# Head pairs, 128-key chunks and a hand-written issue order in a soft-cap attention followed by gated attention experts

## The chip, the cores and the metric

The kernel runs on one core of a Trainium2 chip, in one launch. The metric is the device time of an execution in microseconds (us). Most executions of a kernel agree within 0.3%. TensorE matmuls are called PE, its weight loads PEld, VectorE DVE, ScalarE ACT, GpSimd POOL and SyncE SP.

## The reference

q, k and v are (8, 12, 448, 64), batch, head, position, feature; the output is (8, 448, 768).

```
scores = (q @ k.T) / 8                       # per batch and head
scores = 30 * tanh(scores / 30)
x      = softmax(scores) @ v                 # heads side by side: (8, 448, 768)

logits = x @ w_gate                          # 4 experts, the best 2 of each token
w      = softmax over the two chosen logits
for e in range(4):
    qe, ke, ve = x @ wq[e], x @ wk[e], x @ wv[e]        # 64 wide
    a   = softmax(causal(qe @ ke.T / 8))
    out += (w of e, 0 where not chosen) * (a @ ve @ wo[e])
```

The first part is called stage A, the second stage B. All four experts are computed for all tokens; the weight of an expert that was not chosen is 0.

## The kernel before, in words

Positions go in four chunks of 112. Stage A has 96 iterations, one for a head (batch b, head h, t = 12 b + h). `a_prep` transposes q and k, padded from 64 to 96 features, in eight PE transposes into one PSUM tile, and DVE copies them out. `a_qkt` makes the scores with keys on the partitions: four matmuls of 448 query columns into a score tile of four PSUM banks, of which there is one. `a_tanh` and `a_exp` are one ACT activation each over 112 partitions x 1792 columns. `a_pv` runs 16 matmuls with 112x112 weights (the probabilities) and 65 moving columns (v and a column of ones, which gives the row sum), and DVE normalises.

Stage B of a batch is 18 closures in the list `bq`: x transposed and the gate (`b_xt_gate`), V of all experts (`b_vproj`), then per expert the projection (`b_proj`: Q and K side by side in 128 weight columns), the scores, the causal mask added by a second matmul, one exp over all 448 x 448 (`b_attn`, in the same score tile as stage A), and PV, normalising and the transpose of the result (`b_pv_o`), then four output blocks (`b_out`). They come into the list when the batch is done in stage A, and `pump_bq` takes one out in each iteration, two in every third:

```
        pump_bq(None, 2 if h % 3 == 1 else 1)
        a_qkt(t + 1)
        if t < NH:
            a_exp(t)
    while bq:
        pump_bq(None, 1)
```

PSUM has eight banks: four for the score tile, and four buffers of one bank each (`ps_aux`) which everything else shares. q, k and v of a batch are loaded by three DMAs from the GpSimd queue that convert f32 to f16 on the way (`load_batch`); the weights by 17 such DMAs ahead of them. Each engine takes its instructions in the order in which its queue has them. The functions stand here with the line numbers of the profile.

## Time and profile before

| | |
|---|---|
| median of three runs | 691.7 us (687.6 to 695.7) |
| span of the profiled execution | 686.8 us |
| PE / PEld / DVE / ACT / POOL busy | 538.4 / 408.7 / 261.1 / 372.9 / 124.1 us |
| mean granted TensorE clock | 0.767 |

The profiled execution's time is known by its span, from the first instruction to the last; the runs are timed from outside. PE's busy time is modelled, matmuls overlap in it, so spacings of starts are the safer reading. The granted clock is a share of 2.4 GHz; it takes two levels, 0.5 (1.2 GHz) and 1.0, and before the first recorded change the column shows 1.00 whatever the level.

### The profile page before, as it was taken

How to read it: one execution, taken by the hardware profiler on the slowest of the kernel's cores; microseconds unless marked ns; L12 is line 12 of the kernel's file. 1: busy time of each engine (PE TensorE's matmuls, PEld its weight loads, DVE VectorE, ACT ScalarE, POOL GpSimd, SP SyncE). 2: the span in 40 equal slices, each digit the busy share in tenths (PEclk: the TensorE clock that was granted, in tenths of full speed). 3: DMA queues.
4: the chain of work that ended last, by engine and by line, in shares of the span. 5: the costliest groups of instructions: out<-in, count | busy, mean ns of one | idle time of the engine just before them, and what ended most of it. 6: DMA issues, size and time to landing. Idle time of an engine off the chain costs nothing.

```text
span 686.8 us, 10320 instructions
## 1 busy us (share of the span) xinstructions
PE 538.4 (78%) x4416; PEld 408.7 (60%) x4416; DVE 261.1 (38%) x696; ACT 372.9 (54%) x233; POOL 124.1 (18%) x181
## 2 busy tenths in 40 slices
...
GB/s 80 105 128 22 59 64 1 1 73 112 18 1 52 59 93 1 0 91 72 42 2 81 40 82 1 82 41 21 62 1 1 0 21 62 0 0 81 1 0 81
DMA packets 144062, 29.76 MB, mean 43 GB/s; under 512 B 140177, under 2 KB 140433, under 8 KB 144017
## 3 DMA queue, kind: packets, MB, share of 16 engines
...
## 4 chain that ended last, share of the span: by engine, by line
PE 65%; ACT 17%; DVE 5%; POOL 4%; DMA 4%; issue 4%; DVEq 0%; POOLq 0%; ACTq 0%
PE score L143 13%; PE pv L176 13%; PE qkp L272 8%; ACT pTB L303 8%; PE wops L353 7%; ACT y L155 5%; PE scoreB L288 5%; ACT pT L163 5%; PE pvB L318 4%; PE tps L123 3%; PE tps L128 3%; PE vps L255 3%; PE otp L340 2%; DMA out_dram<-osb 2%; DMA k<-in_k_dram 2%
## 5 line engine op out<-in xcount | busy, mean ns | idle before, releaser
L155 ACT ACTIVATE y<-score 112x1792 f16<-112x1792 f32 x96 | 159.4, 1661 | 154.9 <-PE score L143 154.7
L163 ACT ACTIVATE pT<-y 112x1792 f16<-112x1792 f16 x96 | 162.6, 1694 | 2.0
L143 PE MATMUL score<-qkT 96*112 96x448 f16 x384 | 130.4, 473 | 32.7 <-ACT pTB L303 31.5
L176 PEld LDWEIGHTS <-pT 112*112 112x112 f16 x1536 | 125.2, 174 | 37.5 <-ACT pT L163 30.4
L176 PE MATMUL pv<-v,pT 112*112 112x65 f16 x1536 | 129.6, 251 | 12.0 <-ACT pT L163 11.9
L303 ACT ACTIVATE pTB<-scoreB 112x1792 f16<-112x1792 f32 x32 | 53.2, 1663 | 123.8 <-PE scoreB L295 123.8
L143 PEld LDWEIGHTS <-qkT 96*112 96x112 f16 x384 | 62.4, 175 | 62.7 <-issue 53.8
L187 DVE RECIPROCAL rcp<-pv 112x4 f32<-112x4 f32 x96 | 17.5, 183 | 202.7 <-PE pv L176 202.6
L123 PE MATMUL tps<-ident,q 112*96 112x112 f16 x384 | 69.7, 267 | 29.5 <-POOL v L103 29.5
L134 DVE COPY qkT<-tps 96x896 f16<-96x896 f16 x96 | 59.1, 616 | 48.4 <-PE tps L128 41.6
L123 PEld LDWEIGHTS <-q 112*96 112x96 f16 x384 | 58.2, 169 | 29.6 <-POOL v L103 29.5
L128 PE MATMUL tps<-ident,k 112*96 112x112 f16 x384 | 68.5, 264 | 4.5 <-DMA k<-in_k_dram 4.5
L278 POOL MEMSET qT<- 32x448 f16 x32 | 14.9, 464 | 294.8 <-PE scoreB L295 294.5
L272 PE MATMUL qkp<-xT,wqk 128*128 128x448 f16 x192 | 67.8, 516 | 0.0
L353 PE MATMUL wops<-wo,oT 96*112 96x384 f16 x256 | 64.3, 418 | 1.6 <-DVE osb L360 1.6
L128 PEld LDWEIGHTS <-k 112*96 112x96 f16 x384 | 58.8, 169 | 4.8 <-issue 4.8
L288 PE MATMUL scoreB<-qT,kT 96*112 96x448 f16 x128 | 39.3, 390 | 28.1 <-DVE kT L281 20.8
L318 PE MATMUL pvB<-vall,pTB 112*112 112x65 f16 x320 | 32.8, 268 | 23.1 <-ACT pTB L303 23.1
L353 PEld LDWEIGHTS <-oT 96*112 96x112 f16 x256 | 41.4, 171 | 15.2 <-issue 1.6
L318 PEld LDWEIGHTS <-pTB 112*112 112x112 f16 x320 | 30.3, 195 | 27.0 <-ACT pTB L303 27.0
L360 DVE COPY osb<-wops 112x384 f32<-112x384 f32 x64 | 35.0, 555 | 29.5 <-PE wops L353 21.5
L188 DVE TENSOR_TENSOR x<-pv,rcp 112x256 f16<-112x256 f32 x96 | 40.7, 424 | 3.2
...
## 6 DMA issues: line engine op xcount, KB each, us to landing
out_dram<-osb SPq DMA_DIRECT2D x32, 336.0 KB, 2.7
q<-in_q_dram POOLq DMA_DIRECT2D x8, 672.0 KB, 8.9
k<-in_k_dram POOLq DMA_DIRECT2D x8, 672.0 KB, 11.6
v<-in_v_dram POOLq DMA_DIRECT2D x8, 672.0 KB, 12.5
...
```

The lines of the kernel that those rows point to most:

```text
L123: nc.tensor.transpose(tps[0:KPAD, 0, c * CS : (c + 1) * CS], q16[:, h, c, 0:KPAD], ident[0:CS, 0:CS],)
L128: nc.tensor.transpose(tps[0:KPAD, 1, c * CS : (c + 1) * CS], k16[:, h, c, 0:KPAD], ident[0:CS, 0:CS],)
L134: nc.vector.tensor_copy(qkT[0:KPAD, :, :], tps[0:KPAD, :, :])
L143: nc.tensor.matmul(score[0:CS, kc, 0:S], qkT[0:KPAD, 1, kc * CS : (kc + 1) * CS], qkT[0:KPAD, 0, 0:S], start=True, stop=True,)
L155: nc.scalar.activation(yt[0:CS, :, :], score[0:CS, :, 0:S], AF.Tanh, scale=inv_scale_a / capf)
L163: nc.scalar.activation(pT[0:CS, :, :], yt[0:CS, :, :], AF.Exp, scale=capf)
L176: nc.tensor.matmul(pv[:, qc, 0 : Dh + 1], pT[0:CS, kc, qc * CS : (qc + 1) * CS], v16[:, h, kc, 0 : Dh + 1], start=(kc == 0), stop=(kc == N ...
L272: nc.tensor.matmul(qkp[:, :], wqk16[e][:, j, :], xT[:, j, :], start=(j == 0), stop=(j == NDC - 1),)
L288: nc.tensor.matmul(score[0:CS, kc, 0:S], st["kT"][0:KPAD, kc * CS : (kc + 1) * CS], st["qT"][0:KPAD, 0:S], start=True, stop=False,)
L303: nc.scalar.activation(pT[0:CS, :, :], score[0:CS, :, 0:S], AF.Exp, scale=inv_scale_a)
L318: nc.tensor.matmul(pv[:, qc, 0 : Dh + 1], pT[0:CS, kc, qc * CS : (qc + 1) * CS], vall[:, kc, e, 0 : Dh + 1], start=(kc == 0), stop=(kc == qc),
L353: nc.tensor.matmul(wops[:, :], otiles[(b, e)][0:KPAD, tcx * CS : (tcx + 1) * CS], wo16[e][0:KPAD, half * 384 : (half + 1) * 384], start=(e ...
```

## The change

Nearly the whole kernel is rewritten; what is computed stays. Stage A goes by pairs of heads (48 iterations): q and k of both heads lie side by side in 128 partitions, so eight transposes serve two heads. Keys go in three chunks of 128, and the last 64 keys of both heads share a fourth chunk, block-diagonal with zeros (`ktz`, `vtz`). The first group of a pair (`fill0`, `tanh(p, 0)`, `expo(p, 0)`) has four chunks, the second (`fill1`, ...) three. Query blocks are four windows of 128, the last of which overlaps the third by 64; all weights of PV are so 128 columns wide. x is transposed pair by pair in stage A (`a_xt`).

Stage B goes by two pairs of experts. Q, K and output weights are stacked 128 wide for a pair, V of all experts and the gate come in one product of 260 columns, and the scores are only computed and kept where a query can see a key: blocks of 448, 320 and 192 columns side by side, 1984 for a pair of experts, one exp over them. The steps of a batch stand in a table (`tab`) of eight iterations with two places in each: w1 ahead of the pair's second tanh, w2 at the iteration's end; steps 6 and 7 coincide with steps 0 and 1 of the next batch. The two iterations marked "S" put the packed scores and their exp between two halves of stage A's exp.

Loads become plain f32 DMAs from SP, one batch ahead, and GpSimd converts to f16 three pairs ahead (`a_cast`, seven copies a pair). The weights keep their converting DMAs, after the first casts. The scheduler is set to keep the written order (`manual_schedule`). PSUM: four banks of score, two for PV (`ps_pv`), and two buffers of one bank for all else (`ps_aux`), in place of four.

Cut to its core (removed lines are those of the functions above):

```diff
+    HP = H // 2
+    NP = B * HP
...
+    isc = 1.0 / (Dh ** 0.5)
+    QC, QP = 4, 112
+    KC, KM = 3, 384
+    TL = S - KM
+    WIN = (0, 128, 256, S - 128)
...
+    ps_pv = ctx.enter_context(tc.tile_pool(name="ps_pv", bufs=1, space=bass.MemoryType.PSUM))
+    ps_aux = ctx.enter_context(tc.tile_pool(name="ps_aux", bufs=2, space=bass.MemoryType.PSUM))
+    ctx.enter_context(tc.manual_schedule())
...
+    def load(b, groups):
...
+        for g0, gn in groups:
+            h0, h1 = 2 * g0, 2 * (g0 + gn)
+            nc.sync.dma_start(
+                qf[:, h0:h1, :], q[b, h0:h1].rearrange("h (p c) d -> p h (c d)", c=QC)
+            )
+            nc.sync.dma_start(
+                kf[:, h0:h1, :],
+                k[b, h0:h1, 0:KM].rearrange("h (p c) d -> p h (c d)", c=KC),
+            )
+            kt = k[b, h0:h1, KM:S].rearrange("(j two) p d -> two p j d", two=2)
+            nc.sync.dma_start(ktf[0:64, g0 : g0 + gn, :], kt[0])
+            nc.sync.dma_start(ktf[64:128, g0 : g0 + gn, :], kt[1])
+            nc.sync.dma_start(
+                vf[:, h0:h1, :],
+                v[b, h0:h1, 0:KM].rearrange("h (p c) d -> p h (c d)", c=KC),
+            )
+            vt_ = v[b, h0:h1, KM:S].rearrange("(j two) p d -> two p j d", two=2)
+            nc.sync.dma_start(vtf[0:64, g0 : g0 + gn, :], vt_[0])
+            nc.sync.dma_start(vtf[64:128, g0 : g0 + gn, :], vt_[1])
+        staged[b] = (qf, kf, vf, ktf, vtf)
+    load(0, [(0, 1), (1, 1), (2, 2), (4, 2)])
...
+    def a_cast(p):
...
+        k16 = hd.tile([128, KC, 2, Dh], f16, name=f"k16_{p}", tag="k16")
+        nc.gpsimd.tensor_copy(
+            q16, qf[:, h0 : h0 + 2, :].rearrange("p h (c d) -> p c h d", c=QC)
+        )
+        nc.gpsimd.tensor_copy(
+            k16, kf[:, h0 : h0 + 2, :].rearrange("p h (c d) -> p c h d", c=KC)
+        )
+        kt = ktz[b % 2]
+        nc.gpsimd.tensor_copy(kt[0:64, j, 0:Dh], ktf[0:64, j, :])
+        nc.gpsimd.tensor_copy(kt[64:128, j, Dh:128], ktf[64:128, j, :])
+        vv = v16[b % 2]
+        nc.gpsimd.tensor_copy(
+            vv[:, h0 : h0 + 2, :, 0:Dh],
+            vf[:, h0 : h0 + 2, :].rearrange("p h (c d) -> p h c d", c=KC),
+        )
+        vt_ = vtz[b % 2]
+        nc.gpsimd.tensor_copy(vt_[0:64, j, 0, 0:Dh], vtf[0:64, j, :])
+        nc.gpsimd.tensor_copy(vt_[64:128, j, 1, 0:Dh], vtf[64:128, j, :])
+        cast[p] = (q16, k16)
...
+    def a_tr(p):
...
+        for c in range(QC):
             nc.tensor.transpose(
+                tps[:, c * QP : (c + 1) * QP],
+                q16[:, c, :, :].rearrange("p h d -> p (h d)"),
+                ident[0:QP, 0:QP],
+            )
+        nc.tensor.transpose(tps[:, S : S + 128], ktz[b % 2][:, j, :], ident)
+        for c in range(KC):
             nc.tensor.transpose(
+                tps[:, S + 128 * (c + 1) : S + 128 * (c + 2)],
+                k16[:, c, :, :].rearrange("p h d -> p (h d)"),
+                ident,
+            )
+        qt = hd.tile([128, S + 128], f16, name=f"qt_{p}", tag="qt")
+        nc.vector.tensor_copy(qt, tps[:, 0 : S + 128])
+        kk = kz[p % 3]
+        nc.vector.tensor_copy(kk[0:64, 0, :], tps[0:64, S + 128 : S + 512])
+        nc.vector.tensor_copy(kk[64:128, 1, :], tps[64:128, S + 128 : S + 512])
+        qkt[p] = (qt, kk)
...
+    def fill0(p):
...
+                sc[:, c, 0:S], kk[:, 0, 128 * c : 128 * (c + 1)], qt[:, 0:S],
+                start=True, stop=True,
+            )
+        nc.tensor.matmul(sc[:, 3, 0:S], qt[:, S : S + 128], qt[:, 0:S], start=True, stop=True)
+        score[(p, 0)] = sc
+    def fill1(p):
...
+        for c in range(KC):
+            nc.tensor.matmul(
+                sc[:, c, 0:S], kk[:, 1, 128 * c : 128 * (c + 1)], qt[:, 0:S],
+                start=True, stop=True,
+            )
+        score[(p, 1)] = sc
+    y = {}
+    pr = {}
...
+    def tanh(p, g):
...
+        yt = actp.tile([128, n, S], f16, name=f"y{g}_{p}", tag=f"y{g}")
+        nc.scalar.activation(yt, sc[:, 0:n, 0:S], AF.Tanh, scale=isc / capf)
+        y[(p, g)] = yt
+    def expo(p, g, c0=None, c1=None):
+        n = 4 - g
+        yt = y[(p, g)]
+        if (p, g) not in pr:
+            pr[(p, g)] = actp.tile([128, n, S], f16, name=f"p{g}_{p}", tag=f"p{g}")
+        pt = pr[(p, g)]
+        c0 = 0 if c0 is None else c0
...
+    pvs = {}
...
+    def a_pv(p, g):
...
+        for n in range(4):
+            w = WIN[n]
+            for c in range(KC + 1):
+                if c < KC:
+                    lhsT = pt[:, c, w : w + 128]
+                    rhs = v16[b % 2][:, 2 * j + g, c, :]
+                else:
+                    lhsT = p0[:, KC, w : w + 128]
+                    rhs = vtz[b % 2][:, j, g, :]
                 nc.tensor.matmul(
+                    pv[:, g, 65 * n : 65 * n + 65], lhsT, rhs,
+                    start=(c == 0), stop=(c == KC),
                 )
...
+    def a_norm(p):
...
+        nc.vector.reciprocal(rc, pv[:, :, :, 64:65])
+        xk = hd.tile([128, 4, 2, Dh], f16, name=f"xk_{p}", tag="xk")
         nc.vector.tensor_tensor(
+            xk.rearrange("p n g d -> p g n d"),
+            pv[:, :, :, 0:64],
+            rc.broadcast_to((128, 2, 4, Dh)),
             ALU.mult,
         )
...
+    def a_xt(p):
...
+        transpose4(ps, lambda n: xk[:, n, :, :].rearrange("p g d -> p (g d)"))
+        nc.vector.tensor_copy(
+            xT[b][:, j, :].rearrange("m (p c) -> m c p", c=QC),
+            ps[:, 0:S].rearrange("m (c p) -> m c p", c=QC),
+        )
+    st = {}
...
+    def b_v(b, n):
...
+        ps = ps_aux.tile([128, E * Dh + E], f32, name=f"vps_{b}_{n}", tag="aux")
         for j in range(NDC):
+            nc.tensor.matmul(
+                ps, xT[b][:, j, WIN[n] : WIN[n] + 128], wvg[:, j, :],
+                start=(j == 0), stop=(j == NDC - 1)
+            )
+        pse = ps[:, 0 : E * Dh].rearrange("p (e d) -> p e d", d=Dh)
+        if n < 3:
+            nc.vector.tensor_copy(s["vall"][:, n, :, 0:Dh], pse)
+        else:
+            vb = vtB[b % 2]
+            nc.vector.tensor_copy(vb[0:64, 0:E:2, 0:Dh], pse[64:128, 0:E:2, :])
...
+    def b_q(b, r):
...
+        for j in range(NDC):
+            nc.tensor.matmul(
+                ps, wq2[r][:, j, :], xT[b][:, j, :], start=(j == 0), stop=(j == NDC - 1)
+            )
+        qe = bp.tile([128, S], f16, name=f"qe_{b}_{r}", tag="qe")
+        nc.vector.tensor_copy(qe, ps)
+        s["qe", r] = qe
+    def b_k(b, r):
+        ps = ps_aux.tile([128, S], f32, name=f"kps_{b}_{r}", tag="aux")
+        for j in range(NDC):
+            nc.tensor.matmul(
+                ps, wk2[r][:, j, :], xT[b][:, j, :], start=(j == 0), stop=(j == NDC - 1)
+            )
+        kk = kzB[r]
+        nc.vector.tensor_copy(kk[0:64, 0:S], ps[0:64, :])
+        nc.vector.tensor_copy(kk[64:128, S : S + TL], ps[64:128, KM:S])
+        nc.vector.tensor_copy(kk[64:128, S + TL : 2 * S], ps[64:128, 0:KM])
...
+    COL = {(0, 0): 64, (0, 1): 512, (0, 2): 832, (1, 1): 1024, (1, 2): 1344, (1, 0): 1536}
+    def b_fill(b, r):
+        qe = st[b]["qe", r]
+        kk = kzB[r]
+        sc = ps_score.tile([128, 2048], f32, name=f"sB_{b}_{r}", tag="score")
+        nc.tensor.matmul(sc[:, 0:64], kk[:, KM : KM + 128], qe[:, KM:S], start=True, stop=False)
+        nc.tensor.matmul(
+            sc[:, 0:64], ltm2, ident[:, 0:64], start=False, stop=True,
+        )
+        for (e, c), o in COL.items():
+            n = S - 128 * c
+            nc.tensor.matmul(
+                sc[:, o : o + n], kk[:, e * (S + TL) + 128 * c : e * (S + TL) + 128 * (c + 1)],
+                qe[:, 128 * c : S],
+                start=True, stop=False,
+            )
+            nc.tensor.matmul(sc[:, o : o + 128], ltm, ident, start=False, stop=True)
+        st[b]["sc", r] = sc
+    def b_exp(b, r):
+        s = st[b]
+        pb = pB[r]
+        nc.scalar.activation(pb[:, 64:2048], s.pop(("sc", r))[:, 0:1984], AF.Exp, scale=isc)
...
+    def b_pv1(b, e):
...
+        for n in range(4):
+            w = WIN[n]
+            cs = [c for c in range(KC) if 128 * c <= w] if n < 3 else list(range(KC))
+            ops = []
+            for c in cs:
+                o = 64 + COL[(g, c)] + w - 128 * c
+                ops.append((o, s["vall"][:, c, e, :]))
+            if n == 3:
+                ops.append((0, vtB[b % 2][:, e, :]))
+            for i, (o, rhs) in enumerate(ops):
+                nc.tensor.matmul(
+                    pv[:, n, :], pb[:, o : o + 128], rhs,
+                    start=(i == 0), stop=(i == len(ops) - 1),
                 )
+        rc = bp.tile([128, 4, 1], f32, name=f"rcB_{b}_{e}", tag="rcB")
+        nc.vector.reciprocal(rc, pv[:, :, Dh : Dh + 1])
+        sl = bp.tile([128, 4, 1], f32, name=f"sl_{b}_{e}", tag="sl")
+        nc.vector.tensor_tensor(sl, rc, s["wtok"][:, :, e : e + 1], ALU.mult)
+        nc.vector.tensor_tensor(
+            s["osc", r][:, :, g, :], pv[:, :, 0:Dh], sl.broadcast_to((128, 4, Dh)), ALU.mult
...
+    def b_ot(b, r):
...
+        transpose4(ps, lambda n: osc[:, n, :, :].rearrange("p g d -> p (g d)"))
+        oT = bp.tile([128, S], f16, name=f"oT_{b}_{r}", tag="oT", bufs=4)
...
+    def b_wo(b, n):
+        s = st[b]
+        w = WIN[n]
+        lo = 64 if n == 3 else 0
+        ob = outp.tile([128, D], f32, name=f"ob_{b}_{n}", tag="ob")
+        for f in range(2):
+            ps = ps_aux.tile([128, D // 2], f32, name=f"wops_{b}_{n}_{f}", tag="aux")
+            for r in range(2):
                 nc.tensor.matmul(
...
+                ob[lo:128, f * (D // 2) : (f + 1) * (D // 2)], ps[lo:128, :]
+            )
...
+        nc.sync.dma_start(out[b, w + lo : w + 128, :], ob[lo:128, :])
+    a_cast(0)
+    a_cast(1)
...
+    def weights(e):
...
+        nc.gpsimd.dma_start(
+            wk2[r][:, :, g * Dh : (g + 1) * Dh],
+            moe_wk[e].rearrange("(c p) m -> p c m", p=128),
+        )
+        nc.gpsimd.dma_start(wo2[r][g * Dh : (g + 1) * Dh, :], moe_wo[e])
+        if e == 0:
+            nc.gpsimd.dma_start(
+                wvg[:, :, E * Dh : E * Dh + E], moe_w_gate.rearrange("(c p) e -> p c e", p=128)
...
+    def batch_b(b):
...
+        tab = {
+            0: ([f(b_v, b, 0)], [f(b_v, b, 1), f(b_v, b, 2)]),
+            1: ([f(b_v, b, 3)], [f(b_gate, b), f(b_q, b, 0)]),
+            2: ([f(b_k, b, 0)], [("S", b, 0)]),
+            3: ([f(b_q, b, 1)], [f(b_k, b, 1)]),
+            4: ([f(b_pv1, b, 0), f(b_pv1, b, 1)], [("S", b, 1)]),
+            5: (
+                [f(b_pv1, b, 2), f(b_pv1, b, 3)],
+                [f(b_ot, b, 0), f(b_ot, b, 1), f(b_wo, b, 0)],
+            ),
+            6: ([f(b_wo, b, 1)], []),
+            7: ([f(b_wo, b, 2)], [f(b_wo, b, 3)]),
+        }
+        return tab
+    sched = {}
...
+        for s_, (w1, w2) in batch_b(b).items():
+            e_ = sched.setdefault(HP * (b + 1) + 1 + s_, ([], []))
+            e_[0].extend(w1)
+            e_[1].extend(w2)
+    def run(units):
+        for u in units:
+            u()
+    a_tr(0)
+    a_cast(2)
+    weights(0)
+    a_tr(1)
+    fill0(0)
+    last = max(sched)
+    for p in range(last + 1):
+        w1, w2 = sched.get(p, ([], []))
+        sB = [u for u in w2 if isinstance(u, tuple)]
+        w2 = [u for u in w2 if not isinstance(u, tuple)]
+        b, j = divmod(p, HP)
+        if j == 0 and b + 1 < B:
+            load(b + 1, [(0, HP)])
+        if p < NP:
+            tanh(p, 0)
+            fill1(p)
+        if 1 <= p <= NP:
+            expo(p - 1, 1)
+            a_pv(p - 1, 0)
+        a_tr(p + 2)
+        a_cast(p + 3)
+        if 1 <= p < 4:
+            weights(p)
+        run(w1)
+        if p < NP:
+            tanh(p, 1)
+        if not sB:
+            fill0(p + 1)
+            if p < NP:
+                expo(p, 0)
+        else:
+            for _, bb, r in sB:
+                b_fill(bb, r)
+            if p < NP:
+                expo(p, 0, 0, 2)
+            for _, bb, r in sB:
+                b_exp(bb, r)
+            fill0(p + 1)
+            if p < NP:
+                expo(p, 0, 2, 4)
+        if 1 <= p <= NP:
+            a_pv(p - 1, 1)
+            a_norm(p - 1)
+        run(w2)
+        if 1 <= p <= NP:
+            a_xt(p - 1)
```

## Rows read from the trace of the kernel before

**Rows 1.** The page: busy time of each engine; the chain that ended last.

```profile
PE 538.4 (78%) x4416; PEld 408.7 (60%) x4416; DVE 261.1 (38%) x696; ACT 372.9 (54%) x233; POOL 124.1 (18%) x181
...
PE 65%; ACT 17%; DVE 5%; POOL 4%; DMA 4%; issue 4%; DVEq 0%; POOLq 0%; ACTq 0%
```

**Rows 2.** Windows: stretch, length, busy us per engine (instructions), granted clock, DMA share, GB/s.

```profile
40.00:84.00 44.00, 43.92 (x331) 34.34 (x330) 13.53 (x34) 39.67 (x24) 11.06 (x14) 1.00 1.79 61
...
160.00:240.00 80.00, 68.08 (x594) 52.00 (x593) 34.06 (x93) 51.50 (x33) 15.73 (x21) 0.74 0.79 44
268.00:290.00 22.00, 18.72 (x121) 13.23 (x120) 6.48 (x16) 11.63 (x7) 3.50 (x6) 0.50 0.00 1
...
590.00:687.00 97.00, 58.19 (x355) 37.93 (x354) 31.80 (x83) 11.82 (x8) 5.64 (x16) 0.69 0.09 29
```

**Rows 3.** Timeline of PE, 56 to 66 us: start, us, instructions, count.

```profile
56.20 1.66 PE L176 MATMUL pv<-v,pT 112*112 112x65 f16 x16
57.68 0.31 PE L123 MATMUL tps<-ident,q 112*96 112x112 f16 x1
...
59.92 1.67 PE L176 MATMUL pv<-v,pT 112*112 112x65 f16 x16
```

**Rows 4.** Timelines of PE, 83.5 to 90 and 90 to 96 us.

```profile
84.50 1.33 PE L201 MATMUL xtp<-ident,x 112*128 112x112 f16 x12
...
92.77 1.30 PE L272 MATMUL qkp<-xT,wqk 128*128 128x448 f16 x6
93.91 0.92 PE L143 MATMUL score<-qkT 96*112 96x448 f16 x4
94.67 0.97 PE L176 MATMUL pv<-v,pT 112*112 112x65 f16 x16
95.48 0.23 PE L123 MATMUL tps<-ident,q 112*96 112x112 f16 x1
```

**Rows 5.** Groups of weight loads: shapes, count | busy, mean ns | idle before.

```profile
L201 PEld LDWEIGHTS <-x 112*128 112x128 f16 x192 | 12.8, 103 | 3.8 <-issue 1.5
L211 PEld LDWEIGHTS <-xT 128*112 128x112 f16 x192 | 12.7, 132 | 0.6
```

**Rows 6.** Groups of ACT, with what ended the idle time before.

```profile
L163 ACT ACTIVATE pT<-y 112x1792 f16<-112x1792 f16 x96 | 162.6, 1694 | 2.0
L155 ACT ACTIVATE y<-score 112x1792 f16<-112x1792 f32 x96 | 159.4, 1661 | 154.9 <-PE score L143 154.7
...
L219 ACT ACTIVATE eexp<-lg 112x16 f32<-112x16 f32 x8 | 1.5, 183 | 17.1 <-PE lg L211 17.1
```

**Rows 7.** Groups of DVE: three copies out of PSUM.

```profile
L134 DVE COPY qkT<-tps 96x896 f16<-96x896 f16 x96 | 59.1, 616 | 48.4 <-PE tps L128 41.6
...
L360 DVE COPY osb<-wops 112x384 f32<-112x384 f32 x64 | 35.0, 555 | 29.5 <-PE wops L353 21.5 <-DMA out_dram<-osb 6.9
...
L206 DVE COPY xT<-xtp 128x448 f16<-128x448 f16 x48 | 15.2, 379 | 0.8 <-PE xtp L201 0.7
```

**Rows 8.** Groups of POOL.

```profile
L101 POOL MEMSET q<- 112x1536 f16 x8 | 11.1, 1386 | 51.5 <-PE tps L123 29.5 <-PE tps L128 12.5 <-issue 9.4
...
L103 POOL MEMSET v<- 112x48 f16 x8 | 2.5, 318 | 28.3 <-PE pv L176 24.7 <-issue 3.5
...
masks.py:199 POOL TENSOR_SCALAR_AFFINE_SELECT ident<-ident 128x128 f16<-128x128 f16 x1 | 0.3, 287 | 0.1
...
L415 POOL MEMSET const-uint8-127<- 128x1 uint8 x1 | 0.1, 103 | 0.0
```

**Rows 9.** Timeline of ACT, from 560 us on.

```profile
587.35 1.69 ACT L163 ACTIVATE pT<-y 112x1792 f16<-112x1792 f16 x1
```

**Rows 10.** Timeline of ACT, first 40 us; the page: DMA issues.

```profile
37.83 1.66 ACT L155 ACTIVATE y<-score 112x1792 f16<-112x1792 f32 x1 [35.81 <-PE score L143]
...
out_dram<-osb SPq DMA_DIRECT2D x32, 336.0 KB, 2.7
...
v<-in_v_dram POOLq DMA_DIRECT2D x8, 672.0 KB, 12.5
```

More of the change, by code (lines that the diff above doesn't have):

```diff
@@ new lines @@
+    vtB = [const.tile([128, E, Dh + 1], f16, name=f"vtB{i}") for i in range(2)]
+    pB = [const.tile([128, 64 + 1984], f16, name=f"pB{i}") for i in range(2)]
+    for i in range(2):
+        nc.gpsimd.memset(ktz[i], 0.0)
+    for i in range(3):
+        nc.vector.memset(kz[i], 0.0)
+    for i in range(2):
+        nc.vector.memset(v16[i][:, :, :, Dh : Dh + 1], 1.0)
+        nc.vector.memset(vtz[i], 0.0)
+        nc.vector.memset(vtz[i][0:64, :, 0, Dh : Dh + 1], 1.0)
+        nc.vector.memset(vtz[i][64:128, :, 1, Dh : Dh + 1], 1.0)
```

482 lines of the change are left out of this document (152 added, 330 removed).

## The prediction, made before the changed kernel ran

> **What bounds the kernel now.** I read the chain first, then the stretches. The chain is 65% PE and 17% ACT, while PE is busy 538 of 687 us and ACT 373 [rows 1]: no engine is full over the whole span, so the stages must be looked at apart. From 40 to 84 us only stage A runs, and PE is busy 43.9 of 44 us, ACT 39.7 [rows 2]. A head takes 3.72 us from one PV to the next, and the 16 PV matmuls 1.48 us, 92 ns each [rows 3]; later the same 16 take 0.81 us, 51 ns each [rows 4]. So TensorE ran at the lower of its two levels (1.2 GHz) before and at the upper (2.4 GHz) after. The clock column of the first stretch says 1.00, but the spacing decides. From 160 to 240 us PE has 68 of 80 us, ACT 51.5, clock 0.74; at 268 to 290 us it is 0.50 with PE busy 18.7 of 22 [rows 2]. ACT's tanh waits 154.7 us for PE's scores [rows 6]. Two ends lie outside this: ACT's first tanh begins at 37.8 us [rows 10], and its last stage-A exp ends at 589.0 [rows 9], 97.8 us before the end; in 590 to 687 us ACT is busy 11.8 and PE 58.2 [rows 2]. That tail is the queue's backlog: 18 closures come in per batch, 16 are pulled.
>
> **ACT per pair.** Both activations cover 1792 columns. From 16 columns in 183 ns to 1792 in 1661 [rows 6] one column costs 0.832 ns and the rest 170 ns. A pair now has tanh over 1792 (1.66) and 1344 columns (170 + 1344 x 0.832 = 1.29), exp over 1792 (1.69) and 1344 (1.32): 5.96 us, where two heads took 6.71. 48 pairs: 286 us. Stage B's exp covers 1984 columns for two experts (1.82 us) in place of two of 1792 columns; the split exp beside it adds 0.17. Fourteen of the sixteen, and seven gate exps of 0.18, stand between stage-A work: 14 x 1.99 + 1.3 = 29 us.
>
> **PE.** Columns that stream, per pair: transposes 960, scores 7 x 448, PV 32 x 65, x transposes 512: 6,688. Per batch stage B adds 24 x 260 (V and gate), 2 x 5,376 (Q, K), 2 x 2,816 (packed scores and masks), 40 x 65, 1,024 and 16 x 384: 32,392. Six matmuls of 448 columns start 1.14 us before what follows, 190 ns each [rows 4], so the upper level is 2.36 columns per ns; the lower is half of it, 1.2. A pair costs 2.8 or 5.6 us, a batch with its stage B (72,520 columns) 30.7 or 60.4; ACT needs 6 x 5.96 + 2 x 1.99 + 0.18 = 39.9. PV goes by its weight loads: 112 columns in 92 ns is 1.2 per ns [rows 3]. But weights of 128 columns load in 103 ns where 112 take 132 [rows 5]. So I price the 128-wide PV by its 65 columns, 28 ns; the bound above is 53 ns (128 columns at 2.4 GHz), which adds 32 x 25 ns = 0.8 us a pair of PE time that ACT covers.
>
> The level decides. In rows it stayed low through 44 us of full PE on 96- and 112-wide tiles, and was up by 94.67 us, after the stretch with the 128-wide x transposes from 84.5 us [rows 2, 4]. Every tile of the new kernel is 112 or 128 rows by 128 columns, and stage A alone brings 6,688 columns in 5.96 us, 1,120 per us, against 3,728 in 3.72 us, 1,000, of smaller tiles. I take the upper level; 60.4 us a batch goes into the range.
>
> The first of [rows 4] are transposes, and they ran just ahead of the rise. The Trainium skill, TensorE: Matmul & The Clock Gate, Part 4, says that transposes don't engage the full clock, as they don't count as busy in the same way; by that stage A's transposes, 1,472 of 6,688 columns, would not hold the level up, which is the second rival below; this trace speaks against it but doesn't isolate it.
>
> **DVE and the two shared buffers.** f16 copies out of PSUM: 379 ns for 448, 616 for 896, so 0.142 us + 0.53 ns per element; f32: 555 ns for 384, so 1.08 ns [rows 7]. A pair: 0.45 + 2 x 0.35 (transposed Q, K), 0.15 + 0.69 (normalising), 0.38 for x^T: 2.4 us (2.6 if the strided x^T copy runs at f32's rate). Stage B per batch: V 2.4, gate 1.5, Q 1.2, K 2.8, normalising 2.8, O^T 0.8, output 4.4: 16.0. So 30 of 40 us: DVE fits in sum, not in each iteration. All copies pass through `ps_aux`, now two buffers where there were four, and PE works in written order: a matmul that waits for a buffer holds up the score fill behind it, and ACT waits for that. With matmul times at 2.36 columns per ns I followed one batch's six iterations, each from the end of its first tanh (time 0). ACT then has group 1's exp and tanh until 2.7 us and a four-chunk exp of 1.69 behind them, which hides a fill of 0.95 with its latency: the fill must begin by 3.4. PE does group 1's fill until 0.75, PV until 1.5, transposes until 1.9, and DVE's copies of these end at 3.1. Steps 0 and 6: w1 is two output halves (PE 0.32, DVE 0.55 each) and a V product (0.65, 0.6); the second half gets the transposes' buffer at 3.15, V gets the first half's at 3.7, and the fill begins at 4.35: 0.95 us late. Steps 1 and 7 in the same way, 0.75 late, and Q's copy stands behind the gate's ten small operations, so the next fill is 0.65 late. Step 2: Q's late buffer holds up the transposes, then K's matmuls (1.15), its copies (1.4) and the packed fill (1.4) must all end before the exp of stage B, and only half an exp of 0.9 is there to hide them: 2.9 us. Step 4: the packed fill alone against the half exp, 0.75. Step 5: two output halves end the iteration, 0.4. Step 3: nothing. Together 6.4 us a batch, 45 us in seven. Bounds: 0, if the waits overlap; 16.0 us a batch, if all of stage B's DVE work comes to stand in ACT's way.
>
> **POOL.** No row shows its copies. A pair has seven, over 1,536 elements. Nearest rows: 1,386 ns for 1,536 memset columns (0.83 net), 287 ns for 128 elements of a select, (287 - 103)/128 = 1.4 with the smallest memset's 103 ns as the base, and 318 ns for 48 strided ones, 4.5 [rows 8]. With 0.1 us for each of the seven that is 2.0, 2.9 or 7.6 us a pair; I take 2.9, since a copy also reads. It is done an iteration ahead and hidden under 5.96 us; without that cover it is the third rival. Behind the casts on POOL stand the weight DMAs and V's ones, both needed iterations later.
>
> **Loads.** SP issues a batch one batch ahead; its first cast is wanted three iterations on, some 24 us. Before, each of a batch's three DMAs landed 12.5 us or less after its issue by the median [rows 10]: hidden if they still overlap, at most 3 x 12.5 - 24 = 13.5 us late a batch if they don't, which is 95 us in seven and the range's upper end. SP's output DMAs stand ahead of the next load only when it was long issued. I take 3 us once, when weights share the start.
>
> **Ends.** Start: 336 KB land 2.7 us after issue [rows 10]; a pair's 0.69 MB take 4 to 6, two casts 5.8, transposes, copies and a low-clock fill 2.7: first tanh at 13 us (10 to 20). Tail: batch 7's stage B alone. From the last exp: PV, normalising and x^T 5; four V, three old output blocks and the gate on DVE 8.5; K and its fill 3; exp 2; second exp behind PV and fill 6; O^T and the eight output copies 7.5; last DMA 2.7: 35 us (30 to 45).
>
> **Sum.** 13 + 3 + 286 + 29 + 45 + 35 = 411 us of span. The profiled span is 686.8 and the median of the runs 691.7, so 5 us lie around it: 416 us.
>
> **Rivals.** (1) The buffers bind: every stage-B copy in ACT's way, 7 x (16.0 - 6.4) = 67 more, 483 us; for it speak the halved buffers and the strict order, against it that most steps have slack. (2) The clock stays low: seven batches at 60.4 us plus the 6.4 of waits are 468, the first batch 36, ends 16 + 45, and 5: 570 us. For it: 268 to 290 us; against it the tile sizes. (3) POOL binds: at 4.5 ns per element 7.6 us a pair, hardly over the 47/6 = 7.8 us that an iteration with stage B takes; near 430 us, inside my forecast's own spread. (4) Slower than before: the same casts, dearer. 48 pairs must then take 699 - 56 = 643 us, 13.4 a pair, which needs (13.4 - 0.7)/1.536 = 8.3 ns per element, nearly twice the dearest POOL row: some 700 us or more. (5) The change doesn't do what it says: the stalls vanish altogether and ACT never waits, 370 us.
>
> **How the numbers follow.** Forecast (385 to 450, with rival 3 in it) 0.62; rival 1 (450 to 500) 0.17; rival 2 (500 to 590) 0.10; rival 5 (under 385) 0.07; rival 4 0.04. The range 385 to 500 leaves out 0.21, so I draw it to 380 and 505. About 1% is what a measurement here can tell from no change. Faster by over 1% is all but rival 4 and a corner of it: 0.95; within 1% 0.01; slower 0.04.
>
> **What the changed profile would show.** Right: ACT busy near 320 us and about 80% of the span; tanh waits under 1 us outside the iterations of the table's steps 0 to 2 and 4; PE clock at 1.00 nearly throughout, PV 28 ns apart; first tanh near 13 us, under 45 us after the last stage-A exp; POOL under 3.5 us a pair. Wrong: clock at 0.5 in stage A (rival 2); DVE or the two buffers named in most of PE's waits and iterations of 9 us and more (rival 1); transposes waiting for POOL (3, 4); PE waiting for SP's loads at each batch's start.

## The result, and the profile after

The changed kernel takes 442.3 us (median of 4 runs, 441.0 to 443.2), the kernel before 693.7 beside it (687.6 to 695.9): a ratio of 0.639, 95% interval 0.635 to 0.643. The forecast was 416 us, the range 380 to 505. The profiled execution took 441.8 us with a span of 440.0, so 1.8 us lie around the span. Single executions of some kernels came some per cent slower at a lower granted clock; they count in the medians given here, but not in the ratios and their intervals.

The page of the kernel after, busy time and chain, to be read against [rows 1]:

```profile
PE 311.9 (71%) x3568; PEld 205.7 (47%) x3568; DVE 276.6 (63%) x693; ACT 305.7 (69%) x231; POOL 132.8 (30%) x374
...
PE 45%; DVE 29%; ACT 10%; SPq 6%; issue 5%; DMA 3%; POOL 1%; DVEq 0%; ACTq 0%; POOLq 0%
```

PE lost 227 us of busy time and DVE holds 29% of the chain where it held 5%. Windows of the kernel after: a stretch of stage A alone, one with both stages, the tail (columns as in [rows 2]):

```profile
16.00:36.00 20.00, 14.94 (x135) 9.56 (x135) 8.07 (x18) 17.41 (x13) 18.47 (x39) 1.00 1.35 248
...
160.00:240.00 80.00, 59.18 (x691) 39.52 (x689) 53.20 (x133) 59.16 (x46) 22.71 (x68) 0.96 0.44 134
...
402.00:440.00 38.00, 25.21 (x181) 13.55 (x177) 23.30 (x65) 3.87 (x3) 0.00 (x0) 0.84 0.20 74
```

With both stages the granted clock is 0.96 where it was 0.74, and PE is no longer full; nor is ACT. Groups of the kernel after, each shape by itself:

```profile
L215 ACT ACTIVATE y<-s 128x1792 f16<-128x1792 f32 x48 | 79.8, 1663 | 33.7 <-PE s L195 33.5
L226 ACT ACTIVATE p<-y 128x1344 f16<-128x1344 f16 x48 | 63.3, 1318 | 0.0
L215 ACT ACTIVATE y<-s 128x1344 f16<-128x1344 f32 x48 | 61.9, 1291 | 19.9 <-PE s L202 19.8
L389 ACT ACTIVATE pB<-sB 128x1984 f16<-128x1984 f32 x16 | 29.2, 1824 | 46.2 <-PE sB L383 46.2
...
L136 POOL CAST q<-qf 112x512 f16<-112x512 f32 x48 | 29.5, 614 | 205.1 <-PE tps L164 176.8 <-issue 24.4 <-DMA qf<-in_q_dram 3.4
L139 POOL CAST k<-kf 128x384 f16<-128x384 f32 x48 | 24.4, 509 | 0.4 <-DMA kf<-in_k_dram 0.4
...
L281 DVE COPY xT<-xtp 128x448 f16<-128x448 f16 x48 | 55.9, 1164 | 11.4 <-PE xtp L270 11.1
```

The prices of single activations came out as forecast (1.66, 1.29, 1.32, 1.82 us). ACT waits 53.3 us for stage A's scores where it waited 154.7 [rows 6], and 46.2 more for the packed ones. One price is far off: the x^T copy, 1164 ns for the same shapes that took 379 before [rows 7].

The timeline of ACT in the kernel after: the first tanh, one pair without a wait, one iteration each of steps 1 and 2, and the end of the stream (start, length, and in brackets the idle time before). The last row holds two halves of an exp, 399.50 to 401.65:

```profile
11.66 1.66 ACT L215 ACTIVATE y<-s 128x1792 f16<-128x1792 f32 x1 [9.64 <-PE s L195]
...
37.19 1.66 ACT L215 ACTIVATE y<-s 128x1792 f16<-128x1792 f32 x1
38.73 1.33 ACT L226 ACTIVATE p<-y 128x1344 f16<-128x1344 f16 x1
...
42.70 1.68 ACT L215 ACTIVATE y<-s 128x1792 f16<-128x1792 f32 x1
...
211.02 1.66 ACT L215 ACTIVATE y<-s 128x1792 f16<-128x1792 f32 x1 [1.40 <-PE s L195]
...
218.24 0.22 ACT L322 ACTIVATE eexp<-lg 128x16 f32<-128x16 f32 x1 [1.45 <-DVE lg L311]
218.37 1.65 ACT L215 ACTIVATE y<-s 128x1792 f16<-128x1792 f32 x1
...
222.39 1.29 ACT L215 ACTIVATE y<-s 128x1344 f16<-128x1344 f32 x1 [1.17 <-PE s L202]
223.58 0.94 ACT L226 ACTIVATE p<-y 128x896 f16<-128x896 f16 x1
228.09 1.82 ACT L389 ACTIVATE pB<-sB 128x1984 f16<-128x1984 f32 x1 [3.56 <-PE sB L383]
...
231.65 1.66 ACT L215 ACTIVATE y<-s 128x1792 f16<-128x1792 f32 x1 [0.90 <-PE s L195]
...
399.50 2.15 ACT L226 ACTIVATE p<-y 128x896 f16<-128x896 f16 x2
```

Start 11.7 us, stream to 401.65, tail 38.4; before it was 37.8, 551.2 and 97.8 [rows 9, 10]. Of the 246.8 us of span that went, 26 are from the start, 161 from the stream and 59 from the tail.

A pair without a wait takes 42.70 - 37.19 = 5.51 us, where I had added four activations to 5.96: an exp starts 0.12 us before the tanh ahead of it ends (38.73 against 37.19 + 1.66), for here the two work on different groups. The Trainium skill, ScalarE: Activation LUTs, "What ACT_TABLE_LOAD costs", says that back-to-back activations overlap by about 93 ns; this trace agrees with 0.12. In the kernel before, an exp needed the tanh right ahead of it, and started 0.03 us after its end (37.83 + 1.66 [rows 10]); where stage B's exp stood ahead of it instead, it started 0.10 us before that one's end (587.35 [rows 9]):

```profile
39.52 1.70 ACT L163 ACTIVATE pT<-y 112x1792 f16<-112x1792 f16 x1
...
585.79 1.66 ACT L303 ACTIVATE pTB<-scoreB 112x1792 f16<-112x1792 f32 x1 [1.22 <-PE scoreB L295]
```

An iteration's wait is the sum of its brackets between one first tanh and the next: in step 2 here 1.17 + 3.56 + 0.90 = 5.63 us. DVE and PE of the kernel after, within that step:

```profile
220.27 1.30 PE L347 MATMUL qps<-xT,wq 128*128 128x448 f16 x6 [0.97 <-DVE ob L443]
...
222.66 0.62 DVE L351 CAST qe<-qps 128x448 f16<-128x448 f32 x1
...
223.20 1.16 DVE L281 COPY xT<-xtp 128x448 f16<-128x448 f16 x1
223.34 0.36 PE L164 MATMUL tps<-ident,q 112*128 112x112 f16 x4 [0.49 <-DVE qe L351]
...
224.42 1.29 PE L357 MATMUL kps<-xT,wk 128*128 128x448 f16 x6 [0.50 <-DVE xT L281]
...
225.75 0.62 DVE L361 CAST kzB<-kps 64x448 f16<-64x448 f32 x1 [0.49 <-PE kps L357]
...
226.67 0.20 PE L372 MATMUL sB<-qe,kzB 128*128 128x64 f16 x1 [0.95 <-DVE kzB L362]
...
229.96 1.28 PE L191 MATMUL s<-qt,kz 128*128 128x448 f16 x3 [1.91 <-ACT pB L389]
231.03 0.58 PE L195 MATMUL s<-qt 128*128 128x448 f16 x1
231.41 0.37 PE L245 MATMUL pv<-v,p 128*128 128x65 f16 x3
```

It is one chain through both engines: Q's copy, x^T's copy, K, K's copies, the packed fill, its exp, the next fill. And PE comes out of the wait at the lower level: the fill's four matmuls take from 229.96 to 231.41, 1.45 us, at a granted clock of 0.50 (229.96 to 231.5 us); from 217.23 us they took 0.76, at 1.00. The same trace shows what this costs. In three of the seven batches PE came out of the same wait at the upper level; one of them:

```profile
180.90 0.73 PE L191 MATMUL s<-qt,kz 128*128 128x448 f16 x3 [1.91 <-ACT pB L389]
...
181.86 1.66 ACT L215 ACTIVATE y<-s 128x1792 f16<-128x1792 f32 x1 [0.17 <-PE s L195]
```

The next tanh waits 0.17 us there instead of 0.90. In two of these three batches steps 2 and 3 together wait 4.9 us; in the four batches that came back at 0.50 it is 6.4 to 8.4, together 10.5 us more.

### The profile page after: what moved, and what is told of

Its sections match the earlier page's. It is cut to its first block, busy times and chain, and to the rows that moved or that the text cites. A ratio compares the mean times of both kernels' runs of the same rounds, so it can differ in the third digit from the quotient of the medians.

```text
span 440.0 us, 8813 instructions
## 1 busy us (share of the span) xinstructions
PE 311.9 (71%) x3568; PEld 205.7 (47%) x3568; DVE 276.6 (63%) x693; ACT 305.7 (69%) x231; POOL 132.8 (30%) x374
## 4 chain that ended last, share of the span: by engine, by line
PE 45%; DVE 29%; ACT 10%; SPq 6%; issue 5%; DMA 3%; POOL 1%; DVEq 0%; ACTq 0%; POOLq 0%
PE pv L245 8%; PE s L191 6%; ACT pB L389 6%; DVE ob L443 5%; PE kps L357 4%; PE s L202 4%; DVE xT L281 4%; DVE xk L257 4%; PE vps L300 3%; PE sB L378 3%; PE qps L347 3%; PE xtp L270 2%; PE wops L438 2%; DVE kzB L361 2%; DVE kz L180 2%
## 5 line engine op out<-in xcount | busy, mean ns | idle before, releaser
L215 ACT ACTIVATE y<-s 128x1792 f16<-128x1792 f32 x96 | 141.8, 1477 | 53.6 <-PE s L195 33.5
L226 ACT ACTIVATE p<-y 128x1792 f16<-128x1792 f16 (+2 forms) x110 | 147.2, 1339 | 0.0
L245 PEld LDWEIGHTS <-p 128*128 128x128 f16 x1536 | 66.6, 103 | 21.8 <-issue 6.2
L245 PE MATMUL pv<-v,p 128*128 128x65 f16 x1152 | 66.2, 201 | 0.8 <-ACT p L226 0.8
L281 DVE COPY xT<-xtp 128x448 f16<-128x448 f16 x48 | 55.9, 1164 | 11.4 <-PE xtp L270 11.1
L389 ACT ACTIVATE pB<-sB 128x1984 f16<-128x1984 f32 x16 | 29.2, 1824 | 46.2 <-PE sB L383 46.2
L191 PE MATMUL s<-qt,kz 128*128 128x448 f16 x144 | 40.7, 397 | 27.1 <-ACT pB L389 24.9
L245 PE MATMUL pv<-vtz,p 128*128 128x65 f16 x384 | 58.8, 199 | 0.0
L438 PE MATMUL wops<-wo,oT 128*128 128x384 f16 x128 | 32.2, 348 | 18.2 <-DVE kz L180 10.3
L202 PE MATMUL s<-qt,kz 128*128 128x448 f16 x144 | 39.7, 389 | 4.9 <-ACT y L215 4.8
L443 DVE COPY ob<-wops 128x384 f32<-128x384 f32 (+1 forms) x64 | 34.6, 557 | 5.6 <-PE wops L438 4.6
L257 DVE TENSOR_TENSOR xk<-pv,rc 128x512 f16<-128x512 f32 x48 | 33.2, 692 | 1.7
```

The source lines that it names most:

```text
L191: nc.tensor.matmul(sc[:, c, 0:S], kk[:, 0, 128 * c : 128 * (c + 1)], qt[:, 0:S], start=True, stop=True,)
L202: nc.tensor.matmul(sc[:, c, 0:S], kk[:, 1, 128 * c : 128 * (c + 1)], qt[:, 0:S], start=True, stop=True,)
L215: nc.scalar.activation(yt, sc[:, 0:n, 0:S], AF.Tanh, scale=isc / capf)
L226: nc.scalar.activation(pt[:, c0:c1, :], yt[:, c0:c1, :], AF.Exp, scale=capf)
L245: nc.tensor.matmul(pv[:, g, 65 * n : 65 * n + 65], lhsT, rhs, start=(c == 0), stop=(c == KC),)
L257: nc.vector.tensor_tensor(xk.rearrange("p n g d -> p g n d"), pv[:, :, :, 0:64], rc.broadcast_to((128, 2, 4, Dh)), ALU.mult,)
```

## The experiments

Twelve runs. "Wait of a step" is the median over the batches after the first, from ACT's timeline as above.

**The x^T copy in DVE's order.** The first cuts the price of the copy that was so far off.

```
-            xT[b][:, j, :].rearrange("m (p c) -> m c p", c=QC),
-            ps[:, 0:S].rearrange("m (c p) -> m c p", c=QC),
+            xT[b][:, j, :],
+            ps[:, 0:S],
```

> The copy of x^T goes straight, without the reordering of tokens (so positions reach stage B in the order of the transposes; the work is otherwise the same). Theory A (DVE's backlog: the copy takes 1.16 us where 0.38 was priced, and PE's next matmuls stand behind it in the two shared buffers): the copy falls to about 0.38 us, ACT's idle time per batch from 13 us to near the 6.4 us that was worked out, the step 2 iteration from 13 to under 12 us; 395 to 425 us. Rival B (the written order and the count of buffers set the waits, whatever DVE's prices): 437 us or more.

431.0 us (428.1 to 441.1; ratio 0.622, 0.617 to 0.628), between the two expectations. The group of the copy in this kernel:

```profile
L281 DVE COPY xT<-xtp 128x448 f16<-128x448 f16 x48 | 18.7, 390 | 11.2 <-PE xtp L270 10.9
```

37 us of DVE's busy time went and 11 us of the total (14 by the median of its three fastest executions). The waits of steps 0 and 1 stayed at 2.59 and 1.46 us; step 2 went from 5.6 to 4.3. The copy is a term, not the cause of most waits.

**The same with the order kept:** written in order, read from PSUM with a step.

```
-            xT[b][:, j, :].rearrange("m (p c) -> m c p", c=QC),
-            ps[:, 0:S].rearrange("m (c p) -> m c p", c=QC),
+            xT[b][:, j, :].rearrange("m (p c) -> m p c", c=QC),
+            ps[:, 0:S].rearrange("m (c p) -> m p c", c=QC),
```

> The same copy in the other order of loops: it writes x^T in a row and reads PSUM with a step of 112 elements. If the step of the 2-byte writes is what costs, the copy falls to about 0.62 us (f32's rate of 1.08 ns per element) and theory A gives two thirds of the gain of the straight copy. If any step costs the same, the copy stays at 1.16 us and the time at 442.

433.1 us (0.628, 0.625 to 0.630), 9 us less than the change: two thirds of the gain or more. The two intervals overlap, so it can't be told more sharply. The group in this kernel:

```profile
L281 DVE COPY xT<-xtp 128x448 f16<-128x448 f16 x48 | 29.9, 623 | 11.4 <-PE xtp L270 11.1
```

So 390 ns in order, 623 read with a step (f32's rate, the upper end of my bound), 1164 written with a step. The Trainium skill, VectorE: DVE Perf Modes, "What auto-detection actually checks", says that two 16-bit elements go per cycle only if every tensor has step 1. The 623 agree; the 1164 are 541 ns more again and stand in no bound I had.

**The reordering given to PE:** the copy straight, and the queries read with a step of 112 as moving data of the score fills.

```
+        qn = qt[:, 0:S].rearrange("m (c p) -> m p c", c=QC)
-                sc[:, c, 0:S], kk[:, 0, 128 * c : 128 * (c + 1)], qt[:, 0:S],
+                sc[:, c, 0:S], kk[:, 0, 128 * c : 128 * (c + 1)], qn,
```

> x^T is copied straight, and the reordering is done by PE, which reads the moving Q of the score matmuls with a step of 112 columns, so that scores have their columns in the order of tokens. Theory A: the time of the straight copy, if the 448 columns still start every 190 ns; if the step halves PE's rate, a pair's seven score matmuls take 1.3 us more and fills end later, 430 to 460 us.

641.3 us (0.928, 0.923 to 0.934), far above both expectations. The scores of this kernel, as a group and one fill:

```profile
L192 PE MATMUL s<-qt,kz 128*128 128x448 f16 x144 | 116.9, 930 | 25.4 <-ACT pB L391 24.9 <-ACT y L217 0.6
...
212.55 2.43 PE L192 MATMUL s<-qt,kz 128*128 128x448 f16 x3 [1.91 <-ACT pB L391]
214.80 0.94 PE L196 MATMUL s<-qt 128*128 128x448 f16 x1
```

The records have 930 ns a matmul where the change has 390 to 397. By starts, the safer reading, a matmul takes 0.75 us (three from 212.55 to 214.80) where the change takes 0.19 (three from 217.23 to 217.80): four times as long, not twice. With seven in each of 48 pairs that is 188 us, most of the 210 by which this kernel is slower than the one with the straight copy. The step in DVE's read cost 0.23 us a pair.

**Q ahead of the gate in step 1.**

```
-            1: ([f(b_v, b, 3)], [f(b_gate, b), f(b_q, b, 0)]),
+            1: ([f(b_v, b, 3)], [f(b_q, b, 0), f(b_gate, b)]),
```

> In step 1 of the table the Q product stands ahead of the gate, nothing else changes. Theory A says that in step 2 PE's transposes, K and packed fill all wait in a row behind the copy of Q, which stands behind the gate's operations (some 1.9 us on DVE): 1 to 2 us less in each of seven batches, 428 to 436 us. Rival B (K and the packed fill in one iteration are too long whatever comes before): 440 to 443 us.

469.1 us (0.678, 0.676 to 0.681): 27 us worse. In step 2 the wait grew to 8.0 us, all waits for packed scores from 46.2 to 65.9. In the change Q's copy does stand behind the gate's operations, as forecast: Q is done at 221.5 us, its copy starts at 222.66. But DVE does much of the gate while PE multiplies Q (220.27 to 221.5). By the written order of this kernel the gate comes after Q's copy, and delays x^T's, which K needs. K of this kernel in step 2, whose first tanh starts at 230.02 us (218.37 in the change):

```profile
237.26 2.17 PE L357 MATMUL kps<-xT,wk 128*128 128x448 f16 x6 [2.33 <-DVE xT L281]
```

Counted from that tanh, K starts 1.2 us later than in the change, but the exp of the packed scores 3.2 us. The other 2 us are the clock: after the wait of 2.33 us K takes 2.17 us for 1.29, at a granted clock of 0.56, and the packed fill 2.5 for 1.4, at 0.50.

**The packed scores one step later.**

```
-            2: ([f(b_k, b, 0)], [("S", b, 0)]),
-            3: ([f(b_q, b, 1)], [f(b_k, b, 1)]),
+            2: ([f(b_k, b, 0)], [f(b_q, b, 1)]),
+            3: ([f(b_k, b, 1)], [("S", b, 0)]),
```

> The packed scores of the first pair of experts move from step 2, where they follow K's matmuls and copies in the same iteration, to step 3; Q and K of the second pair move ahead. Theory B with the order as its larger half: the 5 to 5.6 us that ACT idles in step 2 become some 2 us, as in step 4: 15 to 25 us less in seven batches, 417 to 427 us. If DVE's backlog is what delays the scores, wherever they stand, the wait moves along with them: 437 to 445 us.

425.4 us (0.615, 0.611 to 0.618): 17 us less. The mean granted clock of the profiled execution rose with it, from 0.94 to 0.96. Step 2's wait is 2.4 us, and the exp of the packed scores in this kernel waits 1.03 where it waited 3.56:

```profile
225.71 1.82 ACT L389 ACTIVATE pB<-sB 128x1984 f16<-128x1984 f32 x1 [1.03 <-PE sB L383]
```

In iteration 5 ACT waits 6.3 us here (2.45 in the change), for the scores of the second batch's first pair. It is POOL, which waits for that batch's V: its load is issued at 29.35 us, behind SP's slow issues, and lands some 13 us later. And before POOL casts the next pair's q, for which PE's transposes and the fill behind them wait, it issues the last weights. POOL and SP of this kernel:

```profile
43.08 0.51 POOL L146 CAST v<-vf 128x384 f16<-128x384 f32 x1 [5.73 <-DMA vf<-in_v_dram]
...
45.68 0.85 POOL L464 DMA_DIRECT2D wvg<-in_moe_wv_dram  x1 [0.21 <-issue]
...
48.76 0.61 POOL L136 CAST q<-qf 112x512 f16<-112x512 f32 x1
```

```profile
20.10 7.45 SPq L82 DMA_DIRECT2D ktf<-in_k_dram  x1
```

**A third `ps_aux` buffer**, PV in one bank and normalised group by group:

```
-    ps_aux = ctx.enter_context(tc.tile_pool(name="ps_aux", bufs=2, ...
+    ps_aux = ctx.enter_context(tc.tile_pool(name="ps_aux", bufs=3, ...
-            pvs[p] = ps_pv.tile([128, 2, 512], f32, name=f"pv_{p}", tag="pv")
+        pv = pvs[(p, g)] = ps_pv.tile([128, 512], f32, name=f"pv{g}_{p}", tag="pv")
```

> A third buffer for everything but scores and PV: PV takes one bank in place of two, and each group is normalised by itself (two more DVE instructions a pair, about 0.3 us). Theory B (two buffers in written order): the idle time of ACT in steps 0 and 1, 2.6 and 1.4 us, which a straight x^T copy left as it was, falls under half, and the time to 405 to 428 us. Theory A (DVE's work itself): 0.3 us x 48 more DVE, 442 to 455 us.

441.5 us (0.640, 0.636 to 0.644), no difference. Steps 0, 1 and 4 did get shorter (2.1, 1.15, 1.2 us), steps 2 and 3 longer (6.9 and 1.9), and the clock fell from 0.94 to 0.87. DVE and the first matmul of the packed fill in step 2 of this kernel:

```profile
225.57 0.45 DVE L177 COPY qt<-tps 128x576 f16<-128x576 f16 x1
...
226.66 0.62 DVE L356 CAST kzB<-kps 64x448 f16<-64x448 f32 x1
...
227.57 0.24 PE L367 MATMUL sB<-qe,kzB 128*128 128x64 f16 x1 [2.12 <-DVE kzB L357]
```

K was multiplied from 224.16 to 225.5 us, but its copies start at 226.66: DVE runs without a gap from 221 us and has normalising and the transposes' three copies first. A buffer more lets PE go ahead; the packed scores still wait for DVE's queue. Their fill starts 8.35 us after the step's first tanh (227.57 against 219.22), as in the change (8.30). That the step got longer is the clock again: after 2.12 us of waiting the fill takes 2.5 us at a granted clock of 0.50, where the change's takes 1.4.

**The kernel before with q and k padded to 128 features** (`KPAD = 96` to `128`), for the clock.

> The kernel before, with its heads padded to 128 features in place of 96; nothing else. Theory C (the level of TensorE's clock goes by how much of the array the tiles fill, and that is where a good part of the gain lies): stage A alone, from 40 to 84 us, goes over to spacings of the upper level, the mean clock from 0.77 to over 0.9, and the time to 590 to 650 us. Rival (the level follows the waits, not the tiles): the clock stays under 0.82 and the time at 680 to 705 us.

632.4 us (0.914, 0.908 to 0.921), 59 us less than the kernel before beside it, inside theory C's range; the mean clock of the profiled execution is 0.855, short of its 0.9. Its window that answers to the first of [rows 2], and PE of the same stretch:

```profile
40.00:84.00 44.00, 32.99 (x337) 24.32 (x337) 14.50 (x36) 39.18 (x24) 13.86 (x13) 1.00 2.66 59
```

```profile
57.95 1.02 PE L176 MATMUL pv<-v,pT 112*112 112x65 f16 x16 [0.81 <-ACT pT L163]
58.81 0.21 PE L123 MATMUL tps<-ident,q 112*128 112x112 f16 x1
```

PE is busy 33.0 of 44 us instead of 43.9, and the unchanged 16 PV matmuls take 0.86 us, 54 ns each, instead of 1.48 [rows 3]. (The clock column reads 1.00 in both.) Wider tiles alone raise the level of stage A, in the old kernel and with nothing else changed. The Trainium skill, TensorE: Matmul & The Clock Gate, Part 4, says that transposes don't engage the full clock. Eight transposes a head don't keep the level down here; whether they or the scores, which were widened with them, raised it no run separates.

**The kernel before with its queue drained faster** (a second closure whenever `h % 2 == 1`).

> The kernel before, with 18 closures pulled per batch in place of 16, so that no backlog builds up. If the tail was the backlog, its 98 us after the last stage-A exp become 50 to 60; the 14 closures now stand in the stream, where part of them hides: 650 to 680 us. If they cost as much in the stream as at the end: 688 to 700 us.

690.5 us (0.999, 0.995 to 1.003). The last stage-A exp of this kernel:

```profile
625.65 1.70 ACT L163 ACTIVATE pT<-y 112x1792 f16<-112x1792 f16 x1
```

The tail is 61.7 us, from 97.8, and the stream 38 longer: here the backlog is only moved. The mean clock fell too, from 0.77 to 0.73 in the profiled executions, so that PE binds the stream is the likely reason but not the only one that fits. That the change's short tail is a gain because its stream has room for the work is argued from this; no run shows it apart.

**Two edits together:** packed scores later, and the x^T copy written in order.

> The packed scores of the first expert pair moved one step later, and the x^T copy writing in order and reading PSUM with a step, both in one kernel. Alone the first took the median from 442.3 to 425.4 us and the second from 442.3 to 433.1. Theory (the two remove different waits, so they add): 442.3 - 16.9 - 9.2 = 416 us, pB's waits of ScalarE on the scores near 25 us or less, step 2's idle time under 2.4 us. Rival (both shorten the same wait in step 2, between x^T's copy and K's copies): nothing is left for the second, 423 to 426 us.

428.4 us (0.617, 0.611 to 0.622): not under the 425.4 of the first edit alone, and above both expectations; the intervals overlap, so no difference between one edit and the two is shown. Step 2's wait fell from 2.4 to 1.9, the total did not follow. The other executions of this kernel had a mean granted clock of 0.91 to 0.93, those of the first edit alone mostly 0.94 to 0.96. The profiled one took 436.4 us (429.0 with the split load below), so its trace can't tell what the shorter copy was lost to; that stays open.

**All three edits:** packed scores later, the copy in order, the third buffer.

> As the kernel with both edits, and with PV in one bank, normalised group by group, and a third ps_aux buffer. Theory (two ps_aux buffers hold the waits that are left in steps 0, 1 and 4; the third buffer alone cut them by 0.5, 0.3 and 0.9 us and lost it again only in steps 2 and 3, where K and the packed scores met; they no longer meet): 8 x 1.7 = 14 us below the kernel with both edits, about 402 us, with the clock at 0.95 or more. Rival (what the third buffer lets TensorE do ahead it pays for by waiting later for the copies of VectorE, and the clock drops with that wait, as it did at 0.871): no gain, 414 to 428 us, clock under 0.93.

395.7 us (0.571, 0.567 to 0.575), 33 us under the two and faster than both kernels. The page and the same two-stage window of this kernel:

```profile
PE 290.4 (74%) x3568; PEld 200.1 (51%) x3568; DVE 262.4 (66%) x789; ACT 303.8 (77%) x231; POOL 132.3 (34%) x374
```

```profile
160.00:240.00 80.00, 60.71 (x779) 42.66 (x778) 55.94 (x165) 67.06 (x52) 25.71 (x77) 0.96 0.44 129
```

The buffer that was worth nothing alone is worth 33 us once K and the packed scores don't meet and the copy is short. The waits of steps 0 to 5 are 1.8, 1.0, 1.4, 1.3, 0.8 and 0, and the mean clock is 0.96 where the buffer alone had 0.87. The third buffer was not run with the copy's edit alone.

**The two edits with later batches' loads in two parts** (`[(0, HP)]` to `[(0, 2), (2, HP - 2)]`).

> As the kernel with both edits, and each later batch's loads issued in two parts, the first two pairs ahead of the other four. Theory (the 6.3 us that ScalarE idles at pair 5 is GpSimd waiting for V of the second batch's first pair, whose load lands 26 us after its first issue because all six pairs of Q and K and the small rows of the tail go ahead of it): that wait shrinks to under 1 us, the total is 5 us less than with both edits alone, and nothing changes after the first batch. Rival (the queue is held by bytes and small rows in all, and twice the number of transfers only puts the same wait at a later pair, or at the next batch): within 2 us of the kernel with both edits.

421.8 us (0.607, 0.602 to 0.613), 6.6 under the two edits; the wait of iteration 5, 5.2 us with the two edits, is gone. The second batch's first tanh follows the exp ahead of it:

```profile
44.53 1.75 ACT L226 ACTIVATE p<-y 128x1792 f16<-128x1792 f16 x1
46.11 1.71 ACT L215 ACTIVATE y<-s 128x1792 f16<-128x1792 f32 x1
```

**All three without the copy's edit**, to see what the copy is worth there.

> The packed scores of the first expert pair one step later and the third ps_aux buffer with PV in one bank, but the x^T copy as the change has it (writing with a step, 1.16 us instead of 0.62). The kernel that also has the copy writing in order took 395.7 us; that edit alone took 9.2 us off the changed kernel, and with the packed scores moved it took nothing off (428.4 against 425.4). Theory (the copy's length is on the path only where K waits for x^T's and the gate's work on VectorE, in steps 0 to 2, and the third buffer lets TensorE go on meanwhile): 396 to 400 us, steps 0 to 2 longer by no more than 0.2 us each. Rival (VectorE is what is left behind each wait once the buffers are enough, so 0.55 us of copy in each of 48 pairs counts in the five or six loaded steps of a batch): 8 x 5 x 0.3 to 0.55 = 12 to 22 us more, 408 to 418 us.

405.6 us (0.585, 0.581 to 0.589), between the two expectations: the copy is worth 9.9 us here, and the third buffer 20 with the packed scores moved (from 425.4). Steps 0, 1 and 3 wait 0.3, 0.1 and 0.6 us longer, step 2 the same, and the tail is 2 us longer.

## Why the prediction was right, and what was off

The terms of the sum, in us:

| term | forecast | measured | from |
|---|---|---|---|
| start | 13 | 11.7 | first tanh |
| 48 pairs of ACT | 286 | 265 | 48 x 5.53, the usual iteration without a wait |
| stage B's exps in the stream | 29 | 28 | 14 x 1.9 and seven gate exps of 0.2 |
| waits (loads 3, steps 45) | 48 | 97 | stream of 390.0 less the two above; the brackets add up to 89 |
| tail | 35 | 38.4 | 401.65 to the end |
| around the span | 5 | 1.8 | 441.8 - 440.0 |

The 8 us between 97 and 89 are overlap that is lost: an iteration of step 0 lasts 8.34 us with 2.59 of waits, 0.2 more than one without, and stage B's exp takes the overlap from its neighbours.

- The bound was read rightly: ACT's stream with PE at the upper level. The mean clock is 0.94 (forecast 1.00 nearly throughout), ACT is busy 306 us, 69% of the span (forecast 320 and about 80%), PV goes 31 ns apart (16 from 213.71 to 214.21 us; forecast 28), and rival 2 is out. That wider tiles raise the level is shown by the padded kernel, which gained 59 us by it; how the 161 us of the stream divide between the clock and PE's fewer instructions no run separates.
- **The term that was mis-sized is the waits.** The places were right (steps 0, 1, 2, 4, 5), the sizes too small, against "6.4 us a batch". By the iterations that the waits fall into: steps 0 and 6 2.6 (forecast 0.95, and the 0.4 of step 5's end, which shows here as 1.19), 1 and 7 1.46 (0.75), step 2 5.6 (2.9, and the 0.65 that step 1 leaves to the next fill, which shows here as 1.17; but there Q's product waits 0.97 us for the copies of an output block, not its copy for the gate), 4 2.1 (0.75), 3 0.9 (none), 5 0.2. That is 12.9 us a batch by the medians and 83 in all seven, since the first stage B had no wait in steps 0 and 1. The first batch added 6.4 (1.5, 1.4, 1.05 and 2.45), where I had 3. So the sign that tanh waits over 1 us only in the named steps failed: three times in the first batch, and twice by 2.04 us in step 3.
- What failed there: I followed the buffers and PE's matmuls with the matmuls' own times, but not DVE's queue, in which a late copy holds up all behind it, nor the lower level that PE came back at after some of step 2's waits (10.5 us in four batches). Step 2 holds over two fifths; moving the packed scores away from K took 17 us out, the largest gain of an edit made alone.
- The copy of x^T was priced at 0.38 us, 0.6 in the bound; it takes 1.16. By itself that is 9 to 14 us of the time, and not the main part of the waits.
- Rival 1 named the right resource. Its 483 us didn't come, as most steps have slack, and buffers alone don't cure it: one more gave nothing until the order was changed, and then 20 us, or 33 with the shorter copy.
- ACT's pair was 0.43 us too dear, 21 us in 48, since activations that don't depend on each other overlap. By luck this hid two fifths of the waits' error; the total is closer than its parts.
- POOL: seven casts take 2.57 us a pair (forecast 2.9); rivals 3 and 4 are out. The loads were late once, not at each batch; but the weight DMAs, which I had as harmless behind the casts, held POOL from 43.99 to 47.03 us of the change between two pairs' casts, in the chain that ends in the 2.45.
- Rival 5 (no stalls, 370): 395.7 with three more edits shows how much of it was to be had.
